# Order of the G/H products in the first chunk, and which engine copies a transposed chunk first

## The chip, the cores and the metric

One core of one Trainium2 chip. The metric is the device time of one execution in microseconds (us). The kernel before takes 830.83 us (median of three runs, 830.83 to 831.05). Below, a load "lands" when the last update of its semaphore (the counter on which others wait for it) comes, and a "stop" or "gap" of TensorE (PE in the traces) is time in which it has no matmul to start. A "slot" is the step f at which a piece of side work is put into the program. PSUM is the memory in which TensorE leaves its results until ScalarE or VectorE takes them out; a bank is a part of it, and an eviction is such a taking out.

## The reference, cut to what matters

Four batches (6016 x 256 each) of cross-covariance attention, followed by a gated feed-forward layer over all 24064 rows:

```python
qn = q / (norm(q, axis=1) + 1e-6); kn = k / (norm(k, axis=1) + 1e-6)
a  = softmax(kn^T @ qn / tau)                    # 256 x 256 per batch
x  = v @ a                                       # 6016 x 256 per batch
out = (sigmoid(x @ w_gate) * (x @ w_val)) @ w_out   # d_ff = 1536
```

The kernel never forms x. As (v @ a) @ w = v @ (a @ w), it computes G = a @ w_gate and H = a @ w_val once per batch and then sigmoid(v @ G) * (v @ H) @ w_out chunk by chunk (12 chunks of up to 512 rows per batch, each in 12 steps f of 128 columns of d_ff).

## The kernel before: the parts that matter

G and H of a batch come from twelve products. `fg` is one of three groups of 512 columns, `w` is gate (0) or val (1), `i` is the half of the 256 rows. Products 0 to 4 of batch 0 run ahead of the loop, products 5 to 11 inside the steps f=0 to f=6 of the first chunk:

```python
gh_order = [(fg, w, i) for fg in range(NFG) for i in range(CB) for w in range(2)]

def gh(b, n, pl=None, tag=None, act=None):
    fg, w, i = gh_order[n]
    ps = (pl or psm).tile([P, FG], FP32, ...)
    for j in range(CB):
        mm(ps, s["e"][i][:, j, :], w_sb[w][fg][:, j, :], ...)
    # even n: ScalarE takes it out of PSUM, odd n: VectorE
```

Only the first two chunks of v in batch 0 are transposed on TensorE (PE), all others by DMA. The second one is transposed during the first chunk:

```python
def transpose_v(b, ci, ps=None, late=None):
    ...
        for n in range(nt * CB):                       # eight 128x128 transposes, one PSUM tile
            nc.tensor.transpose(out=ps[:, n, :], in_=flat[:, ds(n * P, P)], identity=ident_bf)
        half = nt * CB // 2
        nc.vector.tensor_copy(out=vT[:, :half, :], in_=ps[:, :half, :])
        (nc.scalar.copy if late is None else late)(vT[:, half : nt * CB, :], ps[:, half : nt * CB, :])
...
at(7, lambda: transpose_v(0, 1, psm.tile([P, TPC * CB, P], BF16, tag="m", name="ps_tp")))
```

One step f, with two PSUM buffers each for gate and val:

```python
def glu(b, ci, f):
    # four matmuls of 512 columns: gate (2), val (2)
    nc.scalar.activation(out=g_sb, in_=ps_gate, func=ACT.Sigmoid)
    nc.vector.tensor_tensor(out=hT[:, f], in0=ps_val, in1=g_sb, op=ALU.mult)
```

So the gate matmuls of step f+2 need the sigmoid of step f, and its val matmuls need the hT of step f.

Of the kernel before, what the change touches and what calls it, by code (L numbers as in the profile page):

```python
# [10 lines left out]
BF16 = mybir.dt.bfloat16  # L11
# [6 lines left out]
def kernel(  # L18
# [20 lines left out]
    nc = tc.nc  # L39
    P = nc.NUM_PARTITIONS  # L40
# [8 lines left out]
    CB = C // P  # L49
    FC = DFF // P  # L50
    FG = 512
    NFG = DFF // FG
    TPC = 4
# [12 lines left out]
    def pool(name, bufs, **kw):  # L66
        return ctx.enter_context(tc.tile_pool(name=name, bufs=bufs, **kw))
# [15 lines left out]
    psm = pool("psm", 1, space=PSUM)  # L83
# [26 lines left out]
    t0, nt = groups0[0]  # L110
# [245 lines left out]
            for n in ("G", "H")  # L356
        ]

    gh_order = [(fg, w, i) for fg in range(NFG) for i in range(CB) for w in range(2)]

    def gh(b, n, pl=None, tag=None, act=None):
        s = st[b]
# [20 lines left out]
    def transpose_v(b, ci, ps=None, late=None):  # L383

        t0, nt = groups[ci]
        v_sb = vs.pop((b, ci))
        vT = vtpool.tile([P, TPC * CB, P], BF16, tag="vT", name="vT")
        flat = v_sb[:, :nt, :].rearrange("p t c -> p (t c)")
        if ps is None:
            nc.sync.dma_start_transpose(out=vT[:, : nt * CB, :], in_=flat)  # L390
        else:
            for n in range(nt * CB):
                nc.tensor.transpose(
                    out=ps[:, n, :], in_=flat[:, ds(n * P, P)], identity=ident_bf
                )
            half = nt * CB // 2
            nc.vector.tensor_copy(out=vT[:, :half, :], in_=ps[:, :half, :])
            (nc.scalar.copy if late is None else late)(vT[:, half : nt * CB, :], ps[:, half : nt * CB, :])
        vts[b, ci] = vT.rearrange("p (u cb) n -> p cb u n", cb=CB)

    hts = {}
# [79 lines left out]
    for g, (t0, nt) in enumerate(groups0):  # L481
# [31 lines left out]
    weights(0, 1)  # L513
    late = []
    transpose_v(
        0, 0, psv.tile([P, TPC * CB, P], BF16, tag="v", name="ps_tp"), lambda *a: late.append(a)
    )
# [12 lines left out]
    def side_work(b):  # L530


        side = {}

        def at(slot, fn, *a):
            side.setdefault(divmod(slot, FC), []).append((fn, a))

        for ci in range(NCH):
            nb, nci = (b, ci + 1) if ci + 1 < NCH else (b + 1, 0)
            lb, lci = (b, ci + 2) if ci + 2 < NCH else (b + 1, ci + 2 - NCH)  # L540
            if (nb, nci) == (0, 1):
                at(7, lambda: transpose_v(0, 1, psm.tile([P, TPC * CB, P], BF16, tag="m", name="ps_tp")))
            elif nb < B:
                at(ci * FC + 2, transpose_v, nb, nci)
            if lb < B:
                at(ci * FC + 0, load_v, lb, lci)
        n = b + 1
        if n == B:
            return side
        first, last = (14 if b == 0 else 0), 8 * FC  # L550
        for g, (t0, nt) in enumerate(groups):
            s0 = first + g * (last - first) // NCH
            at(max(0, s0 - 20), load_qk, n, t0, nt)
            for u in range(nt):
                at(first + (t0 + u) * (last - first) // NT, score, n, t0, u)
            if g == 0:
                at(s0, acc_start, n)
            for i, (fn, w) in enumerate(((acc_square, 0), (acc_add, 0), (acc_square, 1), (acc_add, 1))):
                at(s0 + 1 + 2 * i, fn, n, g, w)
        for i in range(6):  # L560
            at(8 * FC + 2 + i, acc_fold, n, *divmod(i, 3))
        at(9 * FC + 9, norms_mm, n)
        for ci, s, *call in (
            (9, 0, wide_sqrt, n),
            (9, 2, wide_inv, n, 0),
            (9, 3, wide_inv, n, 1),
            (10, 0, wide_scale, n),
            (10, 0, exps, n, 0),
            (10, 0, exps, n, 1),
        ):  # L570
            side.setdefault((ci, FC + s), []).append((call[0], call[1:]))
        at(11 * FC + 0, sums_both, n)
        at(11 * FC + 0, gh_tiles, n)
        for i in range(len(gh_order)):
            at(11 * FC + min(i + 1, FC - 1), gh, n, i, *((pss, "s"), (psm, "m"))[i % 2])
        return side
# [3 lines left out]
    for b in range(B):  # L580
        side = side_work(b)
        for ci in range(NCH):
            block = b + 1 < B and ci in (9, 10)
            for f in range(FC):
                glu(b, ci, f)
                flush()
                if prev is not None and not block:
                    out_mms(*prev, f * TPC, (f + 1) * TPC)
                for fn, a in side.get((ci, f), ()):
                    fn(*a)  # L590
                if (b, ci) == (0, 0) and f < len(gh_order) - 5:
                    gh(0, 5 + f, pso, "o")
            if prev is not None and block:
                for s in range(TPC):
                    for fn, a in side.get((ci, FC + s), ()):
                        fn(*a)
                    out_mms(*prev, s * FC, (s + 1) * FC)
                    flush()
            prev = (b, ci)
# [39 lines left out]
```

## Time and profile before

| | before |
|---|---|
| time, median | 830.83 us |
| PE busy | 816.6 of 829.2 us in the profiled run |
| PE waits after 40 us that the profile names | 0.37 us for val weights at f=0, 0.36 us for a sigmoid at f=10 |

The lines are shown in the prediction. PE sets the time; what counts is whether PE has gaps, and gaps are read from the starts of its matmuls.

### The profile page before, as it was taken

Reading aid. Unit: us, or ns where it says so; the run is one execution under the profiler, and the core shown is the slowest. Engines: PE = TensorE matmul, PEld = TensorE weight load, DVE = VectorE, ACT = ScalarE, POOL = GpSimd, SP = SyncE. Lnnn points to the kernel's source line nnn. Section 1 sums busy time; section 2 is a strip of 40 time slices with the busy share of each in tenths; the row PEclk is TensorE's granted clock in tenths of the full one; section 3 lists DMA queues with packets and bytes.
Section 4 is the critical chain, followed back from the end, with each engine's and each line's share of the span. In section 5 each row is a group of like instructions: output and inputs, shape, how many; then the busy total and the mean of one; then the engine's idle time right before and its main releaser. Section 6 shows DMA issues by size and latency. Waiting matters only on the chain.

```text
span 829.2 us, 13794 instructions
## 1 busy us (share of the span) xinstructions
PE 816.6 (98%) x5204; PEld 502.9 (61%) x5218; DVE 588.7 (71%) x1023; ACT 391.6 (47%) x644; POOL 83.0 (10%) x159
## 2 busy tenths in 40 slices
PE   7899999999999999999999999999999999999998
PEld 4546666665666666665575666666566566666666
DVE  6577878787667777778767777777766666666665
ACT  4654444446644444445654444444655444444442
POOL 5532100002110100000211010000000000000000
PEclk9999999999999999999999999999999999999999
DMA  9999623226946433223875352223323423322111
GB/s 210 207 206 208 111 52 81 58 63 125 164 81 130 96 79 65 59 52 78 162 140 121 80 108 62 51 54 85 64 54 63 79 52 82 71 49 67 48 36 72
DMA packets 79028, 77.19 MB, mean 93 GB/s; under 512 B 50801, under 2 KB 55921, under 8 KB 78961
## 3 DMA queue, kind: packets, MB, share of 16 engines
q0 software_dynamic: 23920, 38.81, 28.1%
q1 hardware_dynamic: 54752, 36.91, 17.8%
q8 instruction: 41, 0.67, 0.3%
q10 hardware_dynamic: 288, 0.59, 0.2%
q14 instruction: 27, 0.21, 0.1%
HBM read 78.64 MB, written 24.64 MB: 125 GB/s over the span
## 4 chain that ended last, share of the span: by engine, by line
PE 94%; DMA 4%; DVE 1%; issue 0%; POOL 0%; ACT 0%; POOLq 0%; ACTq 0%
PE ps_o L88 30%; PE ps_gate L88 29%; PE ps_val L88 29%; PE ps_s L88 4%; DMA k_sb<-in_k_dram 3%; PE ps_gh L88 2%; DMA w_val<-in_moe_w_val_dram 1%; DVE hT L423 0%; ACT g_sb L422 0%; DVE sq L176 0%; PE ps_end L88 0%; POOL q_sb L97 0%; PE ps_n L88 0%; POOL w_gate L139 0%; POOL k_sb L97 0%
## 5 line engine op out<-in xcount | busy, mean ns | idle before, releaser
L423 DVE TENSOR_TENSOR hT<-ps_val,g_sb 128x512 bf16<-128x512 f32 (+1 forms) x576 | 390.9, 679 | 207.0 <-ACT g_sb L422 202.6
L422 ACT ACTIVATE g_sb<-ps_gate 128x512 bf16<-128x512 f32 (+1 forms) x576 | 338.2, 588 | 386.3 <-PE ps_gate L88 380.3
L88 PE MATMUL ps_gate<-vT,gh_G 128*128 128x512 bf16 (+1 forms) x1152 | 337.7, 375 | 0.6 <-ACT g_sb L422 0.4
L88 PE MATMUL ps_val<-vT,gh_H 128*128 128x512 bf16 (+1 forms) x1152 | 337.5, 375 | 0.4
L88 PE MATMUL ps_o<-w_out_sb,hT 128*128 128x256 bf16 x2244 | 324.8, 273 | 0.0
L88 PEld LDWEIGHTS <-hT 128*128 128x128 bf16 x2268 | 221.0, 98 | 124.6
L88 PEld LDWEIGHTS <-gh_H 128*128 128x128 bf16 x1152 | 112.7, 98 | 131.7 <-issue 1.4
L88 PEld LDWEIGHTS <-gh_G 128*128 128x128 bf16 x1152 | 112.4, 98 | 38.3 <-issue 0.6
L106 POOL DMA_DIRECT2D v_sb<-in_v_dram x48 | 25.5, 531 | 620.6 <-DMA vT<-v_sb 489.7
L449 DVE COPY out_sb<-ps_o 128x256 f32<-128x256 f32 x187 | 77.3, 413 | 12.6 <-PE ps_o L88 12.6
L88 PE MATMUL ps_s<-k_sb,q_sb 128*128 128x256 bf16 x376 | 66.0, 272 | 5.5 <-DMA k_sb<-in_k_dram 4.4
L88 PEld LDWEIGHTS <-q_sb 128*128 128x128 bf16 x376 | 36.6, 98 | 14.1 <-issue 6.8
L215 DVE TENSOR_TENSOR acc<-acc,sq 128x1024 bf16<-128x1024 bf16 (+1 forms) x66 | 44.1, 669 | 0.0
L176 DVE TENSOR_TENSOR sq<-q_sb 128x1024 bf16<-128x1024 bf16 (+2 forms) x44 | 29.4, 667 | 2.7 <-DMA q_sb<-in_q_dram 2.7
L97 POOL DMA_DIRECT2D q_sb<-in_q_dram x48 | 26.4, 551 | 16.5 <-DMA q_sb<-in_q_dram 8.3
L97 POOL DMA_DIRECT2D k_sb<-in_k_dram x48 | 26.3, 547 | 16.1 <-DMA k_sb<-in_k_dram 8.4
L176 DVE TENSOR_TENSOR sq<-k_sb 128x1024 bf16<-128x1024 bf16 (+2 forms) x34 | 22.4, 658 | 0.8 <-ACT sq L174 0.8
L376 ACT ACTIVATE gh_G<-ps_gh,rrow 128x512 bf16<-128x512 f32 x21 | 14.4, 687 | 12.9 <-PE ps_gh L88 9.1
L88 PE MATMUL ps_busy<-ones_wide,ones_bf 128*128 128x512 bf16 x57 | 16.6, 418 | 1.7 <-DVE shift L127 1.6
L174 ACT ACTIVATE sq<-k_sb 128x1024 bf16<-128x1024 bf16 (+1 forms) x11 | 11.2, 1018 | 14.7 <-DMA k_sb<-in_k_dram 11.9
L378 DVE TENSOR_SCALAR gh_H<-ps_gh,rrow 128x512 bf16<-128x512 f32 x22 | 16.3, 743 | 1.6 <-PE ps_gh L88 1.6
L486 DVE TENSOR_TENSOR acc<-acc,sq 128x1024 bf16<-128x1024 bf16 x16 | 11.1, 692 | 5.7 <-ACT sq L174 5.4
(67 smaller groups left out, 126.4 us busy)
## 6 DMA issues: line engine op xcount, KB each, us to landing
out_dram<-out_sb SPq DMA_DIRECT2D x44, 512.0 KB, 2.9
v_sb<-in_v_dram POOLq DMA_DIRECT2D x44, 256.0 KB, 3.8
q_sb<-in_q_dram POOLq DMA_DIRECT2D x43, 256.0 KB, 7.2
k_sb<-in_k_dram POOLq DMA_DIRECT2D x43, 256.0 KB, 8.1
out_dram<-out_sb SPq DMA_DIRECT2D x3, 384.0 KB, 2.5
w_gate<-in_moe_w_gate_dram POOLq DMA_DIRECT2D x3, 256.0 KB, 6.8
w_val<-in_moe_w_val_dram POOLq DMA_DIRECT2D x3, 256.0 KB, 8.1
w_out_sb<-in_moe_w_out_dram POOLq DMA_DIRECT2D x1, 768.0 KB, 12.7
```

What stands on the lines that cost most here:

```text
L88: nc.tensor.matmul(out, lhsT=lhsT, rhs=rhs, start=start, stop=stop, **kw)
L97: nc.gpsimd.dma_start(out=tl[:, :nt, :], in_=rows(src, b)[:, t0 : t0 + nt, :])
L106: nc.gpsimd.dma_start(out=v_sb[:, :nt, :], in_=rows(v, b)[:, t0 : t0 + nt, :])
L174: nc.scalar.activation(out=sq[:, :nt, :], in_=src[:, :nt, :], func=ACT.Square)
L176: engine.tensor_tensor(out=sq[:, :nt, :], in0=src[:, :nt, :], in1=src[:, :nt, :], op=ALU.mult)
L215: nc.vector.tensor_tensor(out=acc[:, :nt, :], in0=acc[:, :nt, :], in1=st[b]["sq", w][:, :nt, :], op=ALU.add)
L376: nc.scalar.activation(out=dst, in_=ps, func=ACT.Copy, scale=r)
L378: nc.vector.tensor_scalar(out=dst, in0=ps, scalar1=r, scalar2=None, op0=ALU.mult)
L422: nc.scalar.activation(out=g_sb[:, :n], in_=ps_gate[:, :n], func=ACT.Sigmoid)
L423: nc.vector.tensor_tensor(out=hts[b, ci][:, f, :n], in0=ps_val[:, :n], in1=g_sb[:, :n], op=ALU.mult)
L449: nc.vector.tensor_copy(out=out_sb[:, s, :], in_=ps)
L486: nc.vector.tensor_tensor(out=acc[w], in0=acc[w], in1=sq[w], op=ALU.add)
```

## The change

Its intent is to take away two small stops of PE in the first chunk. From group 1 on, both gate products come before both val products, so that the first val product comes one step later. The copy of the transposed chunk is done by ScalarE first, and the transposes move from step 7 to step 8.

```diff
-    gh_order = [(fg, w, i) for fg in range(NFG) for i in range(CB) for w in range(2)]
+    gh_order = [(0, w, i) for i in range(CB) for w in range(2)]
+    gh_order += [(fg, w, i) for fg in range(1, NFG) for w in range(2) for i in range(CB)]
...
             half = nt * CB // 2
-            nc.vector.tensor_copy(out=vT[:, :half, :], in_=ps[:, :half, :])
             (nc.scalar.copy if late is None else late)(vT[:, half : nt * CB, :], ps[:, half : nt * CB, :])
+            nc.vector.tensor_copy(out=vT[:, :half, :], in_=ps[:, :half, :])
...
-                at(7, lambda: transpose_v(0, 1, ...))
+                at(8, lambda: transpose_v(0, 1, ...))
```

More of the change, by code (lines that the diff above doesn't have):

```diff
@@ L396, in transpose_v @@
             half = nt * CB // 2
+            (nc.scalar.copy if late is None else late)(vT[:, half : nt * CB, :], ps[:, half : nt * CB, :])
             nc.vector.tensor_copy(out=vT[:, :half, :], in_=ps[:, :half, :])
-            (nc.scalar.copy if late is None else late)(vT[:, half : nt * CB, :], ps[:, half : nt * CB, :])
         vts[b, ci] = vT.rearrange("p (u cb) n -> p cb u n", cb=CB)
@@ L541, in side_work @@
             if (nb, nci) == (0, 1):
-                at(7, lambda: transpose_v(0, 1, psm.tile([P, TPC * CB, P], BF16, tag="m", name="ps_tp")))
+                at(8, lambda: transpose_v(0, 1, psm.tile([P, TPC * CB, P], BF16, tag="m", name="ps_tp")))
             elif nb < B:
```

## The prediction

> **What bounds the kernel now.** I read the page's totals first, then the chain that ended last, then PE's waits, then the timeline of the two places that the diff touches (first chunk of batch 0, about 39 to 54 us).
>
> ```profile
> span 829.2 us, 13794 instructions
> PE 816.6 (98%) x5204; PEld 502.9 (61%) x5218; DVE 588.7 (71%) x1023; ACT 391.6 (47%) x644; POOL 83.0 (10%) x159
> PE 94%; DMA 4%; DVE 1%; issue 0%; POOL 0%; ACT 0%; POOLq 0%; ACTq 0%
> ```
>
> TensorE is busy 98% of the span and is 94% of the chain. From 40.75 us to the end the chain is almost only matmuls, so a gap removed on PE after 40 us moves everything behind it and ends in the time one to one; work moved between ScalarE and VectorE costs or saves only through such a gap. The whole idle time of PE is 829.2 - 816.6 = 12.6 us, 1.5% of the span, and most of it lies before 40 us in waits for q and k, which the change does not touch: a result over 2% is out of reach from the start. PE's own waits after 40 us are two:
>
> ```profile
> PE ps_gh L88 <- DMA w_val<-in_moe_w_val_dram: 0.4, 1, 0.4
> PE ps_gate L88 <- ACT g_sb L422: 0.4, 1, 0.4
> ```
>
> Their sizes (0.37 and 0.36 us unrounded) count from the modelled end of the matmul before. Starts are the better ruler: two 512-column matmuls in a row take 0.43 us from start to start of the pair where nothing waits. PE's timeline around the two:
>
> ```profile
> 39.78 0.59 PE L88 MATMUL ps_val<-vT,gh_H 128*128 128x512 bf16 x2
> 40.75 0.59 PE L88 MATMUL ps_gh<-w_val,e_sb 128*128 128x512 bf16 x2 [0.37 <-DMA w_val<-in_moe_w_val_dram]
> ...
> 43.41 0.59 PE L88 MATMUL ps_gh<-w_val,e_sb 128*128 128x512 bf16 x2
> ...
> 51.62 0.59 PE L88 MATMUL ps_val<-vT,gh_H 128*128 128x512 bf16 x2
> 52.58 0.59 PE L88 MATMUL ps_gate<-vT,gh_G 128*128 128x512 bf16 x2 [0.36 <-ACT g_sb L422]
> 53.31 0.59 PE L88 MATMUL ps_val<-vT,gh_H 128*128 128x512 bf16 x2
> 53.74 0.59 PE L88 MATMUL ps_gate<-vT,gh_G 128*128 128x512 bf16 x2
> ```
>
> Gap A: 40.75 - (39.78 + 0.43) = 0.54 us. Gap B: 52.58 - (51.62 + 0.43) = 0.53 us, and right behind it 53.31 - (52.58 + 0.43) = 0.30 us; together 0.83 us. What VectorE and ScalarE do ahead of gap B (two timelines, one engine each):
>
> ```profile
> 50.40 0.68 DVE L423 TENSOR_TENSOR hT<-ps_val,g_sb 128x512 bf16<-128x512 f32 x1
> 51.00 0.41 DVE L397 COPY vT<-ps_tp 128x512 bf16<-128x512 bf16 x1
> 52.56 1.29 DVE L423 TENSOR_TENSOR hT<-ps_val,g_sb 128x512 bf16<-128x512 f32 x2 [1.15 <-ACT g_sb L422]
> ...
> 49.65 0.60 ACT L422 ACTIVATE g_sb<-ps_gate 128x512 bf16<-128x512 f32 x1 [0.55 <-PE ps_gate L88]
> 51.44 0.58 ACT L398 COPY vT<-ps_tp 128x512 bf16<-128x512 bf16 x1 [1.19 <-DVE vT L397]
> 51.92 1.09 ACT L422 ACTIVATE g_sb<-ps_gate 128x512 bf16<-128x512 f32 x2
> ```
>
> The transposes start on PE at 49.88 and end at 50.49. VectorE is busy until 51.00, copies its half until 51.41, and only then does ScalarE copy its own. ScalarE idles 1.19 us, and the sigmoid of f=8, whose matmuls start at 50.33 and free it 0.63 us later (the lag of the undisturbed f=7, 49.02 to 49.65), at 50.96, starts only at 51.92 because it stands behind that copy. The gate product of f=10 needs the bank which that sigmoid empties, so PE waits until 52.52; the val product of f=10 needs the hT of f=8, done at 53.25.
>
> **What the Trainium skill says.** "PSUM — Partial Sum Buffer", section "PSUM bank collisions raise a hardware error", says that two engines must not be in one bank at once, reads against reads included. The eight bf16 transposes fill one bank, so the two copies must follow each other in either order; the trace agrees (ScalarE's copy starts 0.03 us after VectorE's ends). "TensorE: Matmul & The Clock Gate", section "Architectural detail", has ScalarE and VectorE as strict FIFO queues; the trace agrees, the ready sigmoid waits about 0.96 us behind the copy. "ScalarE: Activation LUTs", section "What ACT_TABLE_LOAD costs", gives about 1283 ns for the load itself; this trace has 1.28 us (39.69 to 40.97), and it matters below. "Perfetto Trace Analysis", section "Tensor Engine Instruction", says that a matmul's profiled end is a model, which is why I count from starts.
>
> **The change part by part.** The arithmetic and the number of instructions stay; the built program's order shows the moves.
>
> 1. *Order of G/H.* Product number 5 (the first one in the loop, f=0) was the first on val weights 1, which land at 40.71. It becomes the second on gate weights 1, which product 4 has already used before 39.2. So it can start at 40.21, and gap A's 0.54 us go. The first val product is now number 6 at f=1. Per f PE has six 512-column matmuls here, 3 x 0.43 = 1.29 to 1.30 us, so it comes at 40.21 + 1.30 = 41.51, 0.80 us after the weights. The weights of group 2 (issued by 34.7, landing within 6.8 to 8.6 us) are needed from 44.2 on. Saving 0.54 us.
>
> 2. *Does something else hold PE there?* ScalarE's sigmoids cannot start before the table load ends at 40.97, whatever PE does. First sigmoid 40.98 to 41.58, hT 41.61 to 42.30. PE 0.54 earlier wants the gate of f=2 (bank freed by that sigmoid) at 41.94: 0.36 us spare. It wants the val of f=2 (freed by that hT, plus 0.05 of signal) at 42.37 against 42.35: just met. Product 7 at 43.41 is held 0.07 us today by the eviction of product 6 on ScalarE (42.67 + 0.69 = 43.36, same PSUM bank); it moves with product 6 and keeps its 0.07. Val of f=3 is wanted at 43.74 and free at 43.61. From f=4 VectorE has caught up. So nothing is lost in full; I allow 0 to 0.1 us.
>
> 3. *Transposes from f=7 to f=8, ScalarE first.* All times now 0.54 earlier. Gate and val of f=8 come at 49.35 and 49.78 without the 0.45 us of transposes ahead of them. The second val matmul needs the last H piece, evicted by VectorE at 49.74 + 0.74 - 0.54 = 49.94, visible 49.99, wanted at 50.00: maybe 0.05 us lost, as the weight load has to follow it. Transposes 50.2 to 50.9. The sigmoid of f=8 runs at about 50.0, before the copy instead of behind it. ScalarE's copy now waits for PE only: 50.9 to 51.5. VectorE's copy 51.5 to 51.95. Sigmoid f=9 51.4 to 52.0, hT f=9 52.0 to 52.7. PE wants gate f=10 at 51.56 (bank free since 50.6), val f=10 at 51.99 (hT f=8 done 51.3), gate f=11 at 52.42 (sigmoid f=9 done 52.0), val f=11 at 52.85 (hT f=9, 52.75), then chunk 1 at 53.3 with both halves of vT there. No wait of note remains: saving 0.83 us.
>
> 4. *Batches 1 to 3.* They use the same new order in their last chunk before the switch, with all weights long loaded, and ScalarE and VectorE still take turns by number: 12 evictions of 687 and 742 ns as before. First use of group 1 stays four steps into the next batch. Nothing.
>
> Sum: 0.54 + 0.83 - 0.05 to 0.1 = about 1.3 us. 830.83 - 1.3 = 829.5 us.
>
> **The rivals.**
> - *The wait at product 5 only moves.* For: ScalarE and VectorE do nothing before 41 us, and PE, 0.54 us ahead, might run into them (the val of f=2 has 0.02 us spare). Against: step 2, each later need has 0.1 us or more. If it happened, only part 3 would count: 830.0 us.
> - *The two copies still hold something up.* They are serial in either order, and now VectorE's copy could delay the hT of f=9. Against: that hT waits for its sigmoid until 52.0 anyway, and the copy ends by 51.95. If it happened, 0.2 to 0.5 us of gap B stay: 829.8 to 830.0.
> - *The gain is given back later*, by a transfer that bounds the start of batch 1 (DMA queues are full until about 95 us). Against: PE shows no wait for a DMA after 41 us, and the first scores of batch 1 come at 58.7, some 19 us after their loads were issued (37.97 and 39.21), and those land within about 12.4 us. That would leave 830.8 us.
> - *A new stall*, from transposes that now come between val f=8 and gate f=9. It would have to exceed 1.3 us for a slower kernel; I see no candidate.
>
> **Range and chances.** Runs of before lie within 0.22 us. The low end is both gaps in full plus such scatter; the high end is one gap unrealised. 829.0 to 830.3 us. A 2% move is 16.6 us, more than all the idle time of PE, so the same within 2% is near certain.
>
> **What would show it.** Right: PE no longer waits for val weights, product 5 starts about 40.2; ScalarE's vT copy stands ahead of VectorE's, follows the transposes by under 0.1 us, and PE has no wait for a sigmoid near 52; chunk 1 begins 1.3 us earlier, and the last store keeps that lead. Wrong: a new PE wait between 41 and 44 us for ScalarE or VectorE (step 2 fails), one between 50 and 54 (step 3 fails), or the lead shrinking after 54 us (the third rival).

## The result, and the profile after

The changed kernel takes 829.9 us (median of 6 runs, 829.54 to 830.18), the kernel before 830.83 us beside it (6 runs, 830.62 to 831.15). The ratio is 0.9988 with a 95% interval of 0.9975 to 1.0001. The interval contains 1, so these times alone do not settle that there is a gain. Here and below a ratio is the mean time of one kernel's fast runs over that of the other's of the same rounds, so it is not quite the ratio of the medians. The gain is 0.93 us by the medians.

The page of the changed kernel, its span and its totals by engine:

```profile
span 827.9 us, 13794 instructions
PE 817.6 (99%) x5204; PEld 503.5 (61%) x5218; DVE 588.7 (71%) x1023; ACT 391.7 (47%) x644; POOL 83.1 (10%) x159
```

All of PE's waits in the changed kernel (who waited for whom: total us, times, longest us):

```profile
PE ps_s L88 <- DMA k_sb<-in_k_dram: 2.7, 4, 1.2
PE ps_busy L88 <- DVE shift L127: 1.6, 1, 1.6
PE ps_s L88 <- ACT k_sb L130: 1.1, 1, 1.1
PE ps_r L88 <- ACT e_sb L311: 0.2, 1, 0.2
```

Both waits named in the prediction are gone, and no new one has come. PE's timeline at the two places (start, duration, instruction):

```profile
39.64 0.59 PE L88 MATMUL ps_val<-vT,gh_H 128*128 128x512 bf16 x2
40.07 0.59 PE L88 MATMUL ps_gh<-w_gate,e_sb 128*128 128x512 bf16 x2
...
51.40 0.59 PE L88 MATMUL ps_gate<-vT,gh_G 128*128 128x512 bf16 x2
51.84 0.59 PE L88 MATMUL ps_val<-vT,gh_H 128*128 128x512 bf16 x2
52.27 0.59 PE L88 MATMUL ps_gate<-vT,gh_G 128*128 128x512 bf16 x2
```

Product 5 follows at once (40.07 - 39.64 = 0.43 us, the step of an undisturbed pair), and so do the matmuls of f=10 and f=11. ScalarE's timeline, and under it VectorE's, at the same place:

```profile
49.84 0.60 ACT L423 ACTIVATE g_sb<-ps_gate 128x512 bf16<-128x512 f32 x1 [0.27 <-DVE gh_H L379]
50.74 0.59 ACT L398 COPY vT<-ps_tp 128x512 bf16<-128x512 bf16 x1 [0.30 <-PE ps_tp L394]
51.22 0.60 ACT L423 ACTIVATE g_sb<-ps_gate 128x512 bf16<-128x512 f32 x1
```

```profile
49.73 1.44 DVE L424 TENSOR_TENSOR hT<-ps_val,g_sb 128x512 bf16<-128x512 f32 x2
51.36 0.42 DVE L399 COPY vT<-ps_tp 128x512 bf16<-128x512 bf16 x1 [0.20 <-ACT vT L398]
51.86 1.50 DVE L424 TENSOR_TENSOR hT<-ps_val,g_sb 128x512 bf16<-128x512 f32 x2
```

ScalarE now waits for the transposes and not for VectorE. Its sigmoid of f=8 (49.84) is done before the copy.

The two traces can be compared more finely than the two times, and this ruler carries the rest of the document. The first sigmoid of chunk 0 cannot start before its table load is done, with or without the change. From it to the first sigmoid of chunk 1 lies the stretch that the change touches, and from there to the last sigmoid of the kernel the part that must keep the lead. From the starts on ScalarE:

| us | first sigmoid | first of chunk 1 | stretch | from there to the last sigmoid |
|---|---|---|---|---|
| before | 40.98 | 55.23 | 14.25 | 766.07 |
| changed | 40.85 | 53.76 | 12.91 | 766.07 |

The stretch is 1.34 us shorter, and of that nothing is lost in the other 47 chunks. But the medians differ by 0.93 us only. So the profiled run of before was not like most of its runs (it took 831.27 us, more than any of the six timed ones), and this had to be explained.

### The profile page after: what moved, and what is told of

Its sections match the earlier page's. It is cut to its first block, busy times and chain, and to the rows that moved or that the text cites. A ratio compares the mean times of both kernels' runs of the same rounds, so it can differ in the third digit from the quotient of the medians.

```text
span 827.9 us, 13794 instructions
## 1 busy us (share of the span) xinstructions
PE 817.6 (99%) x5204; PEld 503.5 (61%) x5218; DVE 588.7 (71%) x1023; ACT 391.7 (47%) x644; POOL 83.1 (10%) x159
## 4 chain that ended last, share of the span: by engine, by line
PE 94%; DMA 4%; DVE 1%; issue 0%; POOL 0%; ACT 0%; POOLq 0%
PE ps_o L88 30%; PE ps_gate L88 29%; PE ps_val L88 29%; PE ps_s L88 4%; DMA q_sb<-in_q_dram 3%; PE ps_gh L88 2%; DMA w_val<-in_moe_w_val_dram 1%; DVE hT L424 0%; DVE sq L176 0%; PE ps_end L88 0%; ACT g_sb L423 0%; PE ps_n L88 0%; POOL k_sb L97 0%; POOL q_sb L97 0%; PE ps_tp L394 0%
## 5 line engine op out<-in xcount | busy, mean ns | idle before, releaser
L88 PE MATMUL ps_gh<-w_val,e_sb 128*128 128x512 bf16 x44 | 13.4, 379 | 0.2
L88 PEld LDWEIGHTS <-e_sb 128*128 128x128 bf16 x112 | 10.2, 98 | 4.7 <-ACT e_sb L311 0.5
```

Of the source, the lines that this page charges most:

```text
L88: nc.tensor.matmul(out, lhsT=lhsT, rhs=rhs, start=start, stop=stop, **kw)
```

## The experiments

Scatter first: the 31 runs of the kernel before have a median of 830.84 us; 29 lie between 830.49 and 831.30, two at 831.99 and 832.45. All 11 runs of the changed kernel (829.54 to 830.48, those of the repeat below included) lie under the lowest of these 31, 830.49, so that there is a gain is clear from the times. But with intervals of about 0.0013 either way (1 us) no ratio below settles a part of the change by itself, so I read each verdict from the stretch in its trace and quote the times beside it.

### The order of the products alone

```diff
-    gh_order = [(fg, w, i) for fg in range(NFG) for i in range(CB) for w in range(2)]
+    gh_order = [(0, w, i) for i in range(CB) for w in range(2)]
+    gh_order += [(fg, w, i) for fg in range(1, NFG) for w in range(2) for i in range(CB)]
```

> The new G/H order alone, copies and slot as before. My theory (the gaps add): PE's wait for val weights 1 goes (0.54 us by starts), the two gaps at f=10 (0.53 and 0.30) stay; time about 0.5 us under before, ratio 0.9994. Rival (the wait only moves to ScalarE or VectorE): a new PE gap between 41 and 44 us, no gain, ratio 1.0000. Second rival (the saving is all in the order): nearly the whole 0.9 us of the full change.

Measured: 830.6 us (830.43 to 830.71, 5 runs) against 830.74 us, ratio 0.9997 (0.9985 to 1.001). No wait for weights, and the gaps at f=10 as before. PE's timeline of this kernel:

```profile
51.01 0.59 PE L88 MATMUL ps_val<-vT,gh_H 128*128 128x512 bf16 x2
51.97 0.59 PE L88 MATMUL ps_gate<-vT,gh_G 128*128 128x512 bf16 x2 [0.36 <-ACT g_sb L423]
52.69 0.59 PE L88 MATMUL ps_val<-vT,gh_H 128*128 128x512 bf16 x2
```

51.97 - 51.01 - 0.43 = 0.53 us and 52.69 - 51.97 - 0.43 = 0.29 us. The stretch is 13.72 us. Against the first trace of before (14.25) that is the 0.53 us that I had expected, yet the times gained only 0.14 us. No rival fits either: there is no new gap.

### Copies and slot, old order

```diff
-            nc.vector.tensor_copy(out=vT[:, :half, :], in_=ps[:, :half, :])
             (nc.scalar.copy if late is None else late)(vT[:, half : nt * CB, :], ...)
+            nc.vector.tensor_copy(out=vT[:, :half, :], in_=ps[:, :half, :])
-                at(7, lambda: transpose_v(0, 1, ...))
+                at(8, lambda: transpose_v(0, 1, ...))
```

> ScalarE first and slot 8, G/H order as before. Theory: the wait for val weights 1 stays (0.54 us by starts, the size moves with the landing), the gaps at f=10 go: 0.83 us under before, ratio 0.9990. Rival (the copies still hold something up): 0.2 to 0.5 us of gap between f=9 and f=11, ratio 0.9993 to 0.9996.

Measured: 829.92 us (829.58 to 831.29, 5 runs), ratio 0.9992 (0.998 to 1.0005). The stretch is 12.94 us, as short as that of the whole change (12.91). The gaps at f=10 are gone. My expectation missed one thing: with the old order PE should have waited for the val weights at f=0, and it did not (product 5 starts at 40.23, 0.43 us after the pair before). This was the first sign that the wait is not there in every execution.

### The slot alone

```diff
-                at(7, lambda: transpose_v(0, 1, ...))
+                at(8, lambda: transpose_v(0, 1, ...))
```

> Slot 8 alone, VectorE still copies first. Theory (the order of the copies is what counts): ScalarE's copy now ends about 52.8, the sigmoid of f=9 is held behind it until about 52.7, PE waits at f=11 in place of f=10, about 0.41 + 0.30 = 0.7 us; gain about 0.1 us, ratio 0.9999. Rival (the slot is what counts, as the sigmoid of f=8 is out of the way): gaps gone, 0.83 us under before, ratio 0.9990.

Measured: 830.35 us (830.2 to 830.64, 5 runs), ratio 0.9995 (0.9982 to 1.0007). The stretch is 13.61 us. PE's timeline, then ScalarE's:

```profile
51.82 0.59 PE L88 MATMUL ps_val<-vT,gh_H 128*128 128x512 bf16 x2
52.65 0.59 PE L88 MATMUL ps_gate<-vT,gh_G 128*128 128x512 bf16 x2 [0.23 <-ACT g_sb L422]
53.38 0.59 PE L88 MATMUL ps_val<-vT,gh_H 128*128 128x512 bf16 x2
```

```profile
51.51 0.58 ACT L398 COPY vT<-ps_tp 128x512 bf16<-128x512 bf16 x1 [1.09 <-DVE vT L397]
52.00 1.09 ACT L422 ACTIVATE g_sb<-ps_gate 128x512 bf16<-128x512 f32 x2
```

The stop has moved one step on and is 0.40 + 0.29 us: the slot is worth 0.1 us by the stretch (13.72 - 13.61), as expected. The medians differ by 0.39 us (830.74 against 830.35); the rest of it is not in the stretch.

### The order of the copies alone

```diff
-            nc.vector.tensor_copy(out=vT[:, :half, :], in_=ps[:, :half, :])
             (nc.scalar.copy if late is None else late)(vT[:, half : nt * CB, :], ...)
+            nc.vector.tensor_copy(out=vT[:, :half, :], in_=ps[:, :half, :])
```

> ScalarE first alone, slot 7 kept. Theory: ScalarE is idle when the transposes end, copies 50.5 to 51.1, the sigmoid of f=8 follows at once, and no gap is left at f=10: 0.83 us under before, ratio 0.9990, the slot is not needed. Rival (both are needed): a gap of 0.2 us or more stays at f=10, as VectorE's copy then delays the hT of f=8.

Measured: 830.26 us (829.67 to 831.53, 5 runs), ratio 0.9996 (0.9982 to 1.001). The stretch is 12.90 us: all of it, with the slot left at 7. PE's timeline shows steps of 0.43 us through f=10, and ScalarE's shows why:

```profile
51.08 0.59 PE L88 MATMUL ps_val<-vT,gh_H 128*128 128x512 bf16 x2
51.51 0.59 PE L88 MATMUL ps_gate<-vT,gh_G 128*128 128x512 bf16 x2
51.94 0.59 PE L88 MATMUL ps_val<-vT,gh_H 128*128 128x512 bf16 x2
```

```profile
49.98 0.59 ACT L397 COPY vT<-ps_tp 128x512 bf16<-128x512 bf16 x1 [0.28 <-PE ps_tp L393]
50.47 0.60 ACT L422 ACTIVATE g_sb<-ps_gate 128x512 bf16<-128x512 f32 x1
```

The times scatter more than elsewhere (two runs at 829.67 and 831.53) and do not show the 0.8 us by themselves.

### Two PSUM banks in place of the swapped copies

Each half of the transposes gets a PSUM tile of its own, in a bank of its own (the second tile, `ps_tq`, comes from another pool, `pss`; the line that makes the tiles is left out here); both copies still write one vT tile, and VectorE's still stands first in the program.

```diff
+            for n in range(nt * CB):
+                nc.tensor.transpose(out=ps[n // half][:, n % half, :], ...)
+            nc.vector.tensor_copy(out=vT[:, :half, :], in_=ps[0][:, :half, :])
+            nc.scalar.copy(vT[:, half : nt * CB, :], ps[1][:, :half, :])
```

> Old G/H order, slot 7, VectorE's copy first in the program, but the transposes' two halves in two PSUM banks, so that neither copy waits for the other. Theory (the wait between the copies comes from the shared bank and is the cause of the gaps): ScalarE copies at about 50.5, straight after the transposes, the gaps at f=10 go as with the swapped copies, 0.83 us under before. Rival (ScalarE's wait comes from the vT tile that both write): the gaps stay, time as before.

Measured: 829.73 us (829.59 to 830.15, 4 runs) against 830.84 us, ratio 0.9986 (0.9971 to 1.0001); stretch 12.89 us. ScalarE's copy, then VectorE's, then PE at f=10:

```profile
49.89 0.58 ACT L398 COPY vT<-ps_tq 128x512 bf16<-128x512 bf16 x1 [0.28 <-PE ps_tq L394]
```

```profile
50.36 0.41 DVE L397 COPY vT<-ps_tp 128x512 bf16<-128x512 bf16 x1
```

```profile
50.99 0.59 PE L88 MATMUL ps_val<-vT,gh_H 128*128 128x512 bf16 x2
51.42 0.59 PE L88 MATMUL ps_gate<-vT,gh_G 128*128 128x512 bf16 x2
51.85 0.59 PE L88 MATMUL ps_val<-vT,gh_H 128*128 128x512 bf16 x2
```

ScalarE does not wait for VectorE any more, though both write the same vT tile, and both gaps are gone. The shared PSUM tile, which fills one bank, made the wait, and the wait made both gaps. The edit parts the tile and the bank at once, so which of the two it was is not shown; two tiles in one bank were not tried.

### The kernel before, traced again

> The kernel before again, for a second trace of it. After the first four runs I hold that the val weights 1 usually land about 7.4 us after their issue, some 0.2 us before PE wants them, and that the first trace had caught a late landing (8.1 us). Theory (late landing is the exception): no PE wait for val weights at f=0, landing 7.4 us, both gaps at f=10 (0.53 and 0.30 us) as before, profiled time about 830.7. Rival (it is the rule for this kernel, and the other traces with the old order differ for another reason): the wait is there again, 0.5 us, 831.2.

> A third trace of the kernel before. Theory: again no wait for val weights at f=0 (it was in one of the six traces with the old order and the old loads), gaps of 0.52 and 0.29 us at f=10. Rival: the wait is back, so that it is nearer to half of the executions than to one in six.

Measured: 831.06 us and 830.95 us (one run each, their state is unknown; the granted clock was 1.0). Neither trace has a wait for val weights. All the waits of PE after 40 us in the first of them, and its timeline at product 5:

```profile
PE ps_gate L88 <- ACT g_sb L422: 0.4, 1, 0.4
```

```profile
40.02 0.59 PE L88 MATMUL ps_val<-vT,gh_H 128*128 128x512 bf16 x2
40.45 0.59 PE L88 MATMUL ps_gh<-w_val,e_sb 128*128 128x512 bf16 x2
```

From issue to landing of the three val loads, in the first trace of before and in this second one. The middle value is that of val weights 1 (in the first trace they were issued at 32.60 and landed at 40.71, the 8.1 us):

```profile
DMA to landing us min/median/max: 6.8/8.1/8.6
```

```profile
DMA to landing us min/median/max: 6.8/7.4/8.6
```

The stretch is 13.72 and 13.71 us. So the stretch of before is 13.7 us in these two and 14.25 us in the first, and the difference is the late landing. Among the seven traces with the old order and the loads as before (three of before, copies and slot, slot, copies, two banks) the wait is in one. The landing itself can be read in the four traces with the new order and these loads too: it took 7.43 to 7.46 us in ten of the eleven, and 8.11 us in the first.

The trace shows a little more of this landing. A load's semaphore gets 16 updates, and PE waits for the last. In the two repeats fifteen had come by 39.05 and 39.13, the last at 40.26 and 40.20. In the first trace fourteen had come by 38.96, one at 40.04, which is the usual 7.44 us after the issue, and one more at 40.71. So a second update came late, not the usual last one.

Both repeats took about as long as the first trace (their spans are 829.29 and 828.85 us against 829.21) although their stretch is 0.53 us shorter. The rest lies at the start and the end: their first sigmoid came at 41.21 and 41.16 in place of 40.98, and from the last sigmoid to the end of the first repeat it took 8.29 us, against 7.91 in the other two.

### The late landing made on purpose, with the old order and the new

The load of val weights 1 goes behind gate weights 2, in the kernel before and in the changed one:

```diff
-    for fg in range(NFG):
-        for w, src in enumerate((moe_w_gate, moe_w_val)):
+    w_srcs = (moe_w_gate, moe_w_val)
+    for fg, w in ((0, 0), (0, 1), (1, 0), (2, 0), (1, 1), (2, 1)):
+        for src in (w_srcs[w],):
```

> The kernel before with the load of val weights 1 moved one place back, behind gate weights 2: on purpose a landing about 1.3 us later, near 41.3. Theory: PE waits about 1.1 us for it at f=0, time about 1 us above before (ratio 1.0012). Rival (PE's wait is hidden by the table load on ScalarE anyway): under 0.3 us.

> The changed kernel with the same later load. Theory (the new order buys one step of PE, 1.30 us, of slack for these weights): wanted near 41.5, landed near 41.3, no wait or under 0.1 us, time as the changed kernel, about 829.9. Rival: the wait shows at f=1 in the same size, 831.

Measured: old order 832.03 us (831.66 to 832.39, 4 runs), ratio 1.0013 (0.9998 to 1.0028); new order 829.78 us (829.65 to 830.05, 4 runs), ratio 0.9987 (0.997 to 1.0003). The two ranges do not touch, but the two kernels differ in the copies too, so it is the timeline at product 5 that tells of the order. The weights landed at 41.34 and 41.25. PE's timeline of the old order, then of the new:

```profile
39.71 0.59 PE L88 MATMUL ps_val<-vT,gh_H 128*128 128x512 bf16 x2
41.39 0.59 PE L88 MATMUL ps_gh<-w_val,e_sb 128*128 128x512 bf16 x2 [1.08 <-DMA w_val<-in_moe_w_val_dram]
```

```profile
39.75 0.59 PE L88 MATMUL ps_val<-vT,gh_H 128*128 128x512 bf16 x2
40.18 0.59 PE L88 MATMUL ps_gh<-w_gate,e_sb 128*128 128x512 bf16 x2
...
41.48 0.59 PE L88 MATMUL ps_gh<-w_val,e_sb 128*128 128x512 bf16 x2
```

The old order stops for 41.39 - 39.71 - 0.43 = 1.25 us and its stretch is 14.95 us; the new order does not stop and has 12.92 us (about 0.8 us of the difference is the copies'). The order does what it was meant to do, in an execution in which the weights are late.

### The changed kernel again, and a combination

The changed kernel beside more runs of before, and a version with the new order, ScalarE first, slot 7, and the products in the loop taking turns between two PSUM pools:

```diff
-                at(8, lambda: transpose_v(0, 1, ...))
+                at(7, lambda: transpose_v(0, 1, ...))
-                    gh(0, 5 + f, pso, "o")
+                    gh(0, 5 + f, *((pso, "o"), (psm, "m"))[f % 2])
```

> The changed kernel again, beside the kernel before on the same chip. Theory (0.82 us from the copies in every execution, 0.53 us from the order in the few where the weights land late): 0.8 to 1.0 us under before on average, ratio 0.9988 to 0.9990. Rival (the first prediction in full): 1.3 us, ratio 0.9984.

> The new order and ScalarE first, the slot back at 7, and the products in the loop taking turns between two PSUM pools, so that product 7 does not wait for the eviction of product 6 out of the same bank (the 0.08 us left at 42.74 in the changed kernel). Theory: that gap goes, nothing else changes, about 0.08 us under the changed kernel run beside it, within its scatter. Rival (the slot matters once the order is new): a gap of 0.1 us or more at f=10.

Measured: changed kernel 829.96 us (829.64 to 830.48, 5 runs), ratio 0.9989 (0.9977 to 1.0002), stretch 12.94 us. Combination 829.79 us (829.67 to 829.89, 5 runs), ratio 0.9986 (0.9973 to 1.0), stretch 12.82 us; the small stop ahead of product 7 (0.08 us in the changed kernel) is gone and there is none at f=10. It is 0.09 to 0.12 us shorter than the changed kernel in the trace; in the times the two cannot be told apart.

## Why the prediction was right, and where a term of it was too large

The time was inside the range, and the mechanism held, but the sum of 1.3 us had one term that was mis-sized: the 0.54 us of step 1 measured 0.00 us by the stretch where the weights landed at the usual time. That the range held all the same owes something to luck: its high end stood for one gap unrealised, for another reason.

- **What bounds the kernel.** Right. A gap taken from PE in the first chunk ends in the time one to one: the part from chunk 1 to the last sigmoid took 766.07 or 766.08 us in all 13 traces.
- **Step 1, the order of G/H, 0.54 us.** The mechanism is right, and shown by the late load on purpose (1.25 us of wait with the old order, none with the new). The size is wrong as a gain of the typical run. I took the wait from one trace, and that trace had a late landing, 8.1 us. In the other two traces of before it was 7.4 and 7.5 us, and PE did not wait. One trace in seven with the old order shows the wait, and how often it is there in the runs without a trace is not known; the gain in the others is 0.00 us by the stretch (13.72 us with the new order alone, 13.72 and 13.71 us in the repeats of before), and an estimate of the mean gain from these seven is 0.53 / 7 = 0.08 us. Why a second of the load's 16 updates was late in that one execution stays open.
- **Step 2, nothing else holds PE there.** Right: with product 5 at 40.07 there is no new wait up to 44 us, and product 7 keeps the small one, 0.08 us for the 0.07 foretold.
- **Step 3, transposes and copies, 0.83 us.** Right: 13.72 - 12.90 = 0.82 us by the copies alone. What I had not said is that the swap does it all and the slot is not needed. The 0.05 us that I set aside for the last H piece was 0.02 at most: in the changed kernel the transposes start at 50.09, 0.45 us after the val pair of f=8 (49.64), in place of 0.43.
- **Step 4, the other batches.** Right, nothing: no trace differs after chunk 0.
- **The rivals.** The copies hold nothing up, nothing is given back later, and no wait has moved. (I had put the first scores of batch 1 at 58.7; the timeline has them at 58.50, still 6.9 us after their loads landed at 50.37 and 51.62.) None of them named what did happen: that one of the two gaps was not in most traces of the kernel before. I had put the low end at "both gaps in full", and the high end at "one gap unrealised" for a reason that was not the true one.

So the gain of about 0.9 us by the medians is, by the traces, 0.8 us from the order of the copies in every trace and 0.53 us from the order of the products in the one trace in seven in which the weights landed late. The remaining 0.1 us are within the scatter of start and end: over the 13 traces the first sigmoid comes between 40.83 and 41.21, and the part after the last one takes 7.87 to 8.38 us.

## What to carry to other kernels

A wait for a DMA in one trace is one draw: before its size goes into a sum, look at how close the landing is to the need (0.2 us here) and take a second trace. Here two engines emptied one PSUM tile one after the other (ScalarE began 0.03 us after VectorE's end); in such a case let the one go first whose next work the bottleneck waits for, or give each half a tile in a bank of its own. Small effects are better read as the length of a fixed stretch inside the trace than from total times: in the two traces of the changed kernel the stretch agreed within 0.03 us (12.91 and 12.94) though their times differed by 0.58 us (829.90 and 830.48). Where it differed between traces of one kernel, 14.25 against 13.72, PE's timeline showed the stop.

## What the Trainium skill lacked or had wrong

- "DMA: Bandwidth & Descriptors", section "Anatomy of one DMA — SWDGE (gpsimd) path", gives one fit per DMA, about 2.0 us plus the bytes over 436e3 per us. That section has no figure for a load behind others in a full queue, nor for its scatter: the val weights 1 (256 KB written) took 7.44, 7.45 and 8.11 us from issue to landing in three traces of the same kernel, and the 0.7 us of difference decided whether PE waited.
- "TensorE: Matmul & The Clock Gate", section "Back-to-back issue gap", gives about 131 ns per 512-column matmul in a stream with weight loads, and 216 ns for the isolated gap. In every trace here the stream of weight loads and 512-column matmuls keeps 0.43 us per pair, 216 ns each; the measurement decides for the second figure.
